# Block-sparse attention before a routed expert layer: K, Q and V loads issued by ScalarE, gathers issued in two halves, the last ranking step asked for later

## The chip, the cores and the metric

The kernel runs on one core of a Trainium2 chip. The metric is the device time of one execution in microseconds (us), as a median of several runs. The engines are called by these names: PE is TensorE (matmuls, and transposes by a matmul with the identity), DVE is VectorE, ACT is ScalarE, POOL is GpSimd and SP is SyncE, which here only issues transfers. ACT and POOL can issue transfers too. An engine's name with a "q" behind it (SPq) means its instruction queue: the issuing of transfers and the waits ahead of it.

## The reference

All data are float32. First comes block-sparse attention over B = 4 batches, H = 8 heads, S = 768 positions of D = 64 numbers, in blocks of 32 positions. A block of queries sees its own block and the two beside it, the first and the last block of the sequence, and three blocks drawn at random (`sampled_blocks`); queries of the first and last block see everything:

```
scores = where(mask, q @ k.T / sqrt(64), -1e9)
attn   = exp(scores - max); attn /= sum + 1e-9
x      = (attn @ v), heads side by side        # 3072 tokens x 512
```

Then comes a mixture of 8 experts in which each token goes to one expert, chosen by cosine similarity:

```
logits = (x / |x|) @ (emb / |emb|).T / tau
e, gate = argmax(logits), softmax(logits)[argmax]
out    = gate * (relu(x @ w1[e]) @ w2[e])      # w1 512 x 1024, w2 1024 x 512
```

## The kernel before

**Chunks and steps.** The attention is worked off in 24 chunks of 128 queries, six for each batch (`NC` = 6). `attention_fast` (L1206) has a loop over steps s from 0 to 24 (from L1266); b and c are batch and chunk within the batch. Each step scores chunk s, weighs the values of chunk s-1, and makes the logits of chunk s-2. A batch's K and V come in while the batch before is worked on.

In one step PE does, in this order: `score_near` (L502, tile `ac`, L521: scores against the neighbours and the end blocks), `score_far` (L532, tile `dps`, L543: scores against the random blocks), one half of `weigh_near` for chunk s-1 (tile `av`, L578), `turn_x` (L669, tile `xg_ps`), for c from 1 to 4 `turn_k` of one pair of heads of the next batch (L447, tile `kps`, L454, from the raw K rows `kraw`), `weigh_far` of chunk s-1 (L619; `av` out of `vg` and `pd`, L578), `turn_q` of chunk s+1 (L464, L469, from the raw Q rows `qraw`), `chunk_logits` of chunk s-2 (tile `yp`, L685), and the other half of `weigh_near`. In the first chunk of a batch `score_ends` (L553, tile `bps`, L565) is added. PE runs this list strictly in order.

ACT makes the exponentials (`pac` of `ac`, L525 and L529; four of `pd` out of `dps`, L548), every second copy of `kps` (L456), the squares of x (L666) and the copies of the logits (L686). DVE copies the turned Q (L473) and x (L676), part of the gathered K, and normalizes. POOL copies the gathered K (`kg`, L486) and near values into `vg` (L444).

**Loads.** SP issues nearly all transfers, in program order:

- `load_k` (L389) brings the K rows of one pair of heads as two transfers of 192 KB into one of two buffers of `kraw`. In the loop the step with chunk c of batch b loads pair c of batch b+1, which `turn_k` needs in step s+1.
- `load_q` (L380) brings the Q rows of chunk s+3 (256 KB; two transfers where c is 0) into one of three buffers `qraw`. Only the first two chunks' loads stand on ACT.
- `load_v` (L397) names eight parts of the next batch's V; two are loaded in each step with c of 1 to 4.
- `gather_v` (L426, issued at L434) brings the random value blocks of chunk s+1: up to 12 transfers of 64 KB, each from a row offset that SP has read from the tile `offset` (L371) into registers. They go into one of three buffers `vg`; `weigh_far` reads it two steps after the gathers were asked for. In chunk 0 of a batch there are 6.
- Later the stores of x (L776, L782) and the expert weights (L1071).

The body of a step stood in this order: K of the next batch, Q of chunk s+3, all gathers of chunk s+1, V of the next batch, `keep_ends` (L409, a POOL copy) where c is 4, then the scores. The attention is recorded with a schedule by hand: on each engine the instructions stay in the order of the program. A transfer signals its landing on one of eight semaphores that go round over all transfers that SP and ACT issue.

**Experts' embedding and the last ranks.** `build_experts` (L209) is a generator. Its first two parts (square, power, reciprocal, scaling of the embedding) stood before the first gathers; the transposes come in step 1. After the attention, `expert_tiles` (L1368) runs over tiles of 128 tokens, `expert_tile` (L1108) doing two halves of the first product (`hp`, L1118) and the second product (`yp`, L1131). The tokens of the first two batches are dispatched early, the others late. `rank` (L787, product at L794) counts the places of the last batch's tokens; the generator `between` called it, with the first part of `dispatch_late` (L942), after the first expert tile.

Of the kernel before, what the change touches and what calls it, by code (L numbers as in the profile page):

```python
# [20 lines left out]
P = 128  # L21
B, H, S, D = 4, 8, 768, 64
BLK = 32
NB = S // BLK
NRAND = 3
# [8 lines left out]
NE = (EARLY * S - E * (G - 1) + G - 1) // G  # L34
# [331 lines left out]
def shifts(k, engine, s, c):  # L366

    blocks = blocks_of(c)
    key = engine, s, c
    if key not in k.shift:  # L370
        _, values = k.nc.values_load_multi_w_load_instructions(  # L371
            k.offset[0:1, s, NG * c + blocks[0]:NG * c + blocks[-1] + 1], engines=(engine,), min_val=0, max_val=S - BLK,
            skip_runtime_bounds_check_because="the block numbers are clamped to the blocks there are")
        if engine == mybir.EngineType.SP and s == NRAND - 1:
            return list(values)
        k.shift[key] = list(values)
    return k.shift[key]


def load_q(k, n):  # L380

    b, c = divmod(n, NC)
    k.raw["q", n] = t = k.ld.tile([P, H, D], F32, name="qraw", tag="qraw", bufs=3)
    src = k.q[b].rearrange("h s d -> s h d")
    for rows, lo in pieces(c):
        (k.nc.scalar if n < 2 else k.nc.sync).dma_start(out=t[rows], in_=src[lo:lo + rows.stop - rows.start])


def load_k(k, g, pool=None):  # L389

    b, j = divmod(g, NPAIR)
    k.raw["k", g] = t = (pool or k.ld).tile([P, NC, 2, D], F32, name="kraw", tag="kraw", bufs=2)
    for h in range(2):
        k.nc.sync.dma_start(out=t[:, :, h], in_=k.k[b, 2 * j + h].rearrange("(c p) d -> p c d", p=P))  # L394


def load_v(k, b):  # L397
# [11 lines left out]
def keep_ends(k, b):  # L409

    k.nc.gpsimd.tensor_copy(out=k.vg0[b % 2][D:P], in_=k.vst[b % 2][0:D, 0])


def blocks_of(c):

    return range(2 if c == 0 else 0, NG)
# [6 lines left out]
    return slice(lo, lo + BLK), tile // 2  # L423


def gather_v(k, n):  # L426

    b, c = divmod(n, NC)
    k.vg[n] = t = k.vg_ring[n % len(k.vg_ring)]
    src = k.v[b].rearrange("h s d -> s h d")  # L430
    for s in range(NRAND):
        lanes = slice(s * BLK, (s + 1) * BLK)
        for g, shift in zip(blocks_of(c), shifts(k, mybir.EngineType.SP, s, c)):
            k.nc.sync.dma_start(out=t[lanes, g, :, 0:D], in_=src[bass.ds(shift, BLK)])  # L434


def near_v(k, n):
# [768 lines left out]
def attention_fast(n, ctx):  # L1206
    def pool(name, bufs, **kw):
        return ctx.enter_context(n.tc.tile_pool(name=name, bufs=bufs, **kw))

    nc = n.nc  # L1210
    right = ExitStack()
    n.big, n.dp = pool("big_f", 2, space=PSUM), pool("dp_e", 1)
    n.ld, n.qp, n.gp, n.pp, n.pb_pool = pool("ld", 1), pool("qp", 2), pool("gp", 2), pool("pp", 2), pool("pb", 1)
    odd = pool("odd", 1)
    even = right.enter_context(n.tc.tile_pool(name="even", bufs=1, side="right"))
    setup = ExitStack()
    n.setup = setup.enter_context(n.tc.tile_pool(name="setup", bufs=1, side="right"))
    for i, kv in enumerate((even, odd)):
        n.kt[i] = kv.tile([P, NPAIR, S], F32, name=f"kt{i}")
        n.ke[i] = kv.tile([P, NPAIR, D], F32, name=f"ke{i}")  # L1220
        n.vst[i] = kv.tile([P, NC, H, D + 1], F32, name=f"vst{i}")
        n.vg0[i] = kv.tile([P, H, D + 1], F32, name=f"vg0{i}")
    n.zeros = None
    n.vg_ring = [n.gp.tile([P, NG, H, D + 1], F32, name=f"vg{i}", tag=f"vg{i}", bufs=1) for i in range(3)]
    n.qt_ring = [n.qp.tile([P, NPAIR, 2, P], F32, name=f"qt{i}", tag=f"qt{i}", bufs=1) for i in range(2)]
    load_block_ids(n)
    for g in range(NPAIR):
        if g % 2 == 0:
            load_q(n, g // 2)
        load_k(n, g, n.setup if g < 2 else None)  # L1230
    load_experts(n)
    for to, src in load_v(n, 0):
        nc.sync.dma_start(out=to, in_=src)
    warm_up(n, 10)
    for vg in n.vg_ring:
        nc.vector.memset(vg, 0.0)
    nc.scalar.activation(n.setup.tile([P, 1], F32, name="first_exp"), n.zeros[:, 0:1], ACT.Exp)
    build_ident(n)
    for i in range(2):
        nc.gpsimd.memset(n.vst[i][:, :, :, D:D + 1], 1.0)  # L1240
        nc.gpsimd.memset(n.qt_ring[i], 0.0)
    for vg in n.vg_ring:
        nc.gpsimd.memset(vg[:, :, :, D:D + 1], 1.0)
    build_choice(n)
    turn_q(n, 0)
    for g in range(NPAIR):
        turn_k(n, g)
        if g:
            score_ends(n, 0, g - 1)
    score_ends(n, 0, NPAIR - 1)  # L1250
    build_bias(n)
    gather_k(n, 0)
    n.half = n.const.tile([P, NC], F32, name="half")
    nc.vector.memset(n.half, 0.5)
    experts = build_experts(n)
    next(experts)
    next(experts)
    gather_v(n, 0)
    near_v(n, 0)
    keep_ends(n, 0)  # L1260
    zero = n.const.tile([1, XW], F32, name="zero")
    nc.gpsimd.memset(zero, 0.0)
    nc.sync.dma_start(n.x_dram[N:N + 1, :], zero)
    plan = []
    for s in range(NCH + 1):
        b, c = divmod(s, NC)  # L1266
        if c == 1 and b:
            plan = after_sequence(n, b - 1) + [p for p in plan if p[0] >= s]

        def planned(half):  # L1270
            for when, part, what in plan:
                if (when, part) == (s, half):
                    what()

        if s == 0:
            load_q(n, 2)
            for g in range(NPAIR, NPAIR + 2):
                load_k(n, g)
        if b + 1 < B and c >= 2 and NPAIR * (b + 1) + c < B * NPAIR:
            load_k(n, NPAIR * (b + 1) + c)  # L1280
        if s + 3 < NCH:
            load_q(n, s + 3)
        if s + 1 < NCH:
            gather_v(n, s + 1)
        if b + 1 < B and c:
            for to, src in load_v(n, b + 1)[2 * c - 2:2 * c]:
                nc.sync.dma_start(out=to, in_=src)
        if b + 1 < B and c == 4:
            keep_ends(n, b + 1)
        if s < NCH:  # L1290
            score_near(n, s)
            score_far(n, s)
        if s + 1 < NCH:
            gather_k(n, s + 1)
        planned(0)
        if s >= 1:
            weigh_near(n, s - 1, 0)
        if s == 1:
            next(experts)
        ends = range(NPAIR) if c == 0 and 0 < s < NCH else ()  # L1300
        for j in ends[0:2]:
            score_ends(n, s, j)
        if s >= 2:
            turn_x(n, s - 2)
        for j in ends[2:]:
            score_ends(n, s, j)
        if 1 <= c <= NPAIR and b + 1 < B:
            g = NPAIR * (b + 1) + c - 1
            turn_k(n, g)
        if s >= 1:  # L1310
            weigh_far(n, s - 1)
        if s + 1 < NCH:
            near_v(n, s + 1)
            turn_q(n, s + 1)
        if s >= 2:
            chunk_logits(n, s - 2)
        if s == 1:
            next(experts)
        if s >= 1:
            weigh_near(n, s - 1, 1)  # L1320
            normalize(n, s - 1)
        if s == 0:
            build_consts(n)
        if s == 1:
            setup.close()
        if s == NC * (B - 1):
            right.close()
            n.wp = n.wp_ctx.enter_context(n.tc.tile_pool(name="wp", bufs=1, side="right", reuse_waits="tile"))
        planned(1)
# [35 lines left out]
                        pass  # L1365


def expert_tiles(n, between=(), halfway=None, then=None, spread=None):  # L1368
    def first_late():
        if spread:  # L1370
            spread()
        fetch_rows(n, NE)

    between, n.scattered, n.stop = iter(between), None, NE + FULL
    for i in range(NE + FULL):
        if i + 2 == NE:
            for _ in between:
                pass
        fetch(n, i)
        if len(parts(i)) == 2:  # L1380
            mixed_tile(n, i)
        else:
            expert_tile(n, i, first_late if i == NE - 2 else None, *((halfway, then) if i == 0 else ()))
        next(between, None)


# [16 lines left out]
def fast(n):  # L1403
    n.rings, n.loads = {}, 0
    with ExitStack() as ctx:
# [11 lines left out]
        n.dp = pool("dp", 1, reuse_waits="tile")  # L1417
        n.wp2, n.hps = pool("wp2", 1, reuse_waits="tile"), pool("hps", 1, space=PSUM)

        def between():  # L1420
            rank(n, B - 1)
            n.late = dispatch_late(n)
            next(n.late)
            yield
            yield
            next(n.late)
            count_good(n)
            yield
# [4 lines left out]
                for _ in route(n, B - 1):  # L1433
                    pass

        expert_tiles(n, between(), partial(turn_x, n, NCH - 1), last_route, lambda: next(n.late))


def more(n):
# [106 lines left out]
```

## Time and profile before

| | us |
|---|---|
| median of 3 runs (669.15, 669.15, 664.85) | 669.15 |
| the profiled execution | 663.43 |
| its span in the trace | 661.7 |
| first `ac` of the attention | 19.60 |
| first expert matmul | 285.3 |
| PE busy in the span | 609.8 |
| PE busy between 19.60 and 285.30 | 231.1 |
| transfers: median from issue to landing, `vg` / `kraw` / `qraw` / `vst` | 2.9 / 4.6 / 4.4 / 3.8 |

The span is the time from the first to the last instruction; the 1.7 us around it are not in the trace. A line such as "PE kps L454 <- DMA kraw<-in_k_dram: 14.6, 5, 5.4" reads: PE, at line 454 (writing the tile `kps`), waited for the transfer from K in memory to the tile `kraw`, 14.6 us in total, 5 times, 5.4 us at the longest. In the table by windows a row gives the window, its length, the busy time and (in brackets) the number of instructions of PE, PEld (PE's weight loads), DVE, ACT and POOL, then the clock that was granted to PE (1.00 is full), the busy share of the transfer engines and GB/s. The steps begin, by their first `ac`, at 19.6, 25.9, 38.1, 47.1, 56.8, 72.5, 81.0, 94.0, 106.3, 114.7, 124.3, 136.8, 144.4, 159.3, 171.5, 180.2, 196.2, 208.3, 216.1, 228.2, 244.0, 251.5, 259.8 and 269.5 us (steps 0 to 23).

### The profile page before, as it was taken

The page shows a single profiled execution, that of the slowest core. Times are in us where ns is not written, and L with a number is a line of the kernel's source. Part 1 is how long each engine was busy: PE and PEld are TensorE (multiplying, and loading weights), DVE is VectorE, ACT ScalarE, POOL GpSimd, SP SyncE. Part 2 cuts the span into 40 slices and gives each one's busy share as a digit, 9 for nine tenths or more (in the row PEclk, how much of TensorE's full clock was granted, in tenths as well). Part 3 has the DMA queues.
Part 4 walks back from the last instruction along what each step waited for, and adds up shares of the span by engine and source line. Part 5 has one row for each costly group of instructions (what it writes and reads, how often), then busy time and mean ns, then how long its engine had stood idle before and what let it go on. Part 6 is the DMA issues. An engine that isn't in the chain of part 4 may idle for free.

```text
span 661.7 us, 21659 instructions
## 1 busy us (share of the span) xinstructions
PE 609.8 (92%) x9016; PEld 477.6 (72%) x9016; DVE 224.3 (34%) x661; ACT 119.0 (18%) x265; POOL 235.6 (36%) x446
## 2 busy tenths in 40 slices
PE   7797989898968889897999999999999999999995
PEld 4696979797967879785777666774666755766773
DVE  5663335542643657225810211112211211221210
ACT  2523243443224424200000000000000000000000
POOL 1762333543352436203023333344333343333332
PEclk7899789988978989888999999999999999999998
DMA  8856664766667666999999999899899998999711
GB/s 178 172 129 150 148 139 105 176 137 168 145 146 168 161 142 177 245 276 398 374 412 388 349 354 335 313 340 331 309 404 394 409 373 315 406 399 399 281 49 33
DMA packets 189758, 170.80 MB, mean 258 GB/s; under 512 B 150152, under 2 KB 150280, under 8 KB 186834
## 3 DMA queue, kind: packets, MB, share of 16 engines
q1 hardware_dynamic: 182338, 155.36, 73.9%
q0 software_dynamic: 5216, 13.43, 5.7%
q8 instruction: 73, 1.20, 0.8%
q10 hardware_dynamic: 2096, 0.52, 0.4%
q14 instruction: 35, 0.29, 0.1%
HBM read 156.65 MB, written 12.90 MB: 256 GB/s over the span
## 4 chain that ended last, share of the span: by engine, by line
PE 83%; DMA 4%; SPq 4%; issue 3%; DVE 2%; POOL 1%; ACT 1%; POOLq 0%; DVEq 0%; ACTq 0%
PE hp L1118 25%; PE yp L1131 24%; PE av L578 11%; PE dps L543 5%; DMA kraw<-in_k_dram 4%; PE ac L521 3%; PE yp L685 3%; SPq L434 3%; PE hp L1163 2%; PE yp L1183 2%; PE xg_ps L469 2%; PE kps L454 2%; PE bps L565 1%; PE xg_ps L674 1%; SPq L394 1%
## 5 line engine op out<-in xcount | busy, mean ns | idle before, releaser
L1118 PEld LDWEIGHTS hp<-xgt,w 128*128 128x128 f32 x1472 | 169.5, 194 | 10.2 <-issue 10.2
L1118 PE MATMUL hp<-xgt,w 128*128 128x128 f32 x1472 | 170.2, 277 | 0.0
L1131 PE MATMUL yp<-w,h 128*128 128x512 f32 x368 | 162.0, 592 | 0.0
L1131 PEld LDWEIGHTS yp<-w,h 128*128 128x128 f32 x368 | 68.1, 190 | 76.6 <-issue 76.3
L1042 POOL DMA_INDIRECT xg<-x_dram,quarter x88 | 88.6, 1007 | 30.1 <-issue 27.4
L1144 POOL DMA_INDIRECT out_dram<-y,slot_l x20 | 20.3, 1015 | 156.7 <-DVE y L1143 156.7
L486 POOL COPY kg<-kt 128x128 f32 x176 | 44.6, 296 | 77.1 <-issue 46.9
L1121 ACT ACTIVATE h<-hp 128x512 f32<-128x512 f32 x23 | 13.7, 597 | 289.4 <-PE hp L1118 289.4
L444 POOL COPY vg<-vst 32x520 f32<-32x520 f32 x80 | 49.6, 619 | 33.4 <-PE av L578 25.1
L1125 DVE TENSOR_SCALAR h<-hp 128x512 f32<-128x512 f32 x23 | 15.9, 691 | 133.5 <-PE hp L1118 133.5
L578 PE MATMUL av<-vst,pac 64*64 64x65 f32 x1056 | 49.0, 230 | 5.7 <-issue 5.4
L473 DVE COPY qt<-xg_ps 64x512 f32<-64x512 f32 x48 | 33.1, 689 | 61.8 <-PE xg_ps L469 61.0
L543 PE MATMUL dps<-qt,kg 128*64 128x64 f32 x1408 | 49.6, 231 | 0.4 <-issue 0.4
L1143 DVE TENSOR_SCALAR y<-yp,gate 128x512 f32<-128x512 f32 x20 | 15.0, 751 | 102.2 <-PE yp L1131 90.1
L543 PEld LDWEIGHTS dps<-qt,kg 128*64 128x64 f32 x1408 | 46.1, 145 | 2.4 <-issue 0.7
L578 PEld LDWEIGHTS av<-vst,pac 64*64 64x64 f32 x1056 | 41.0, 141 | 5.3 <-issue 3.1
L548 ACT ACTIVATE pd<-dps,bias 128x256 f32<-128x256 f32 x88 | 34.6, 473 | 9.0 <-PE dps L543 8.5
L521 PE MATMUL ac<-qt,ke 64*64 64x128 f32 (+1 forms) x384 | 30.6, 292 | 4.3 <-DVE qt L473 3.8
L578 PE MATMUL av<-vg,pd 128*32 128x65 f32 x1408 | 29.7, 238 | 4.5 <-issue 4.3
L676 DVE COPY xt<-xg_ps 128x512 f32<-128x512 f32 x24 | 16.5, 689 | 44.2 <-PE xg_ps L674 44.2
L578 PEld LDWEIGHTS av<-vg,pd 128*32 128x32 f32 x1408 | 24.8, 120 | 9.1 <-issue 8.3
L454 PE MATMUL kps<-ident,kraw 128*128 128x128 f32 x96 | 16.3, 316 | 15.5 <-DMA kraw<-in_k_dram 15.5
(229 smaller groups left out, 645.8 us busy)
## 6 DMA issues: line engine op xcount, KB each, us to landing
w<-in_moe_w_dram SPq DMA_DIRECT2D x52, 2048.0 KB, 14.5
vg<-in_v_dram SPq DMA_DIRECT2D x264, 64.0 KB, 2.9
kraw<-in_k_dram SPq DMA_DIRECT2D x32, 192.0 KB, 4.6
vst<-in_v_dram SPq DMA_DIRECT2D x20, 256.0 KB, 3.8
qraw<-in_q_dram SPq DMA_DIRECT2D x19, 256.0 KB, 4.4
w<-in_moe_w_dram SPq DMA_DIRECT2D x8, 512.0 KB, 5.4
x_dram<-x SPq DMA_DIRECT2D x4, 774.0 KB
x_dram<-x SPq DMA_DIRECT2D x4, 516.0 KB, 9.6
```

Of the source, the lines that this page charges most:

```text
L444: k.nc.gpsimd.tensor_copy(out=k.vg[n][NRAND * BLK:P, g], in_=k.vst[b % 2][rows, m])
L454: nc.tensor.transpose(ps[:, c // 3, c % 3 * P:(c % 3 + 1) * P], raw[:, c].rearrange("p h d -> p (h d)"), k.ident)
L473: k.nc.vector.tensor_copy(out=t[rows, :, h], in_=ps[rows])
L486: copy(out=t[:, :, g, s * BLK:(s + 1) * BLK], in_=kt[:, :, bass.ds(shift, BLK)])
L521: nc.tensor.matmul(ps[D * r:D * (r + 1), h, lo:lo + cols.stop - cols.start], lhsT=keys, rhs=qt[rows, j, h, cols], start=True, stop=True)
L543: nc.tensor.matmul(out[D * r:D * (r + 1), NG * j + g], lhsT=kg[:, j, g, D * r:D * (r + 1)], rhs=qt[:, j, :, cols], start=True, stop=True)
L548: nc.scalar.activation(e[:, :, g].rearrange("p j h t -> p j (h t)"), out.rearrange("p (j g) h t -> p j g (h t)", g=NG)[:, :, g], ACT.Exp, ...
L578: k.nc.tensor.matmul(av[lanes, h // NPAIR, h % NPAIR * P:h % NPAIR * P + D + 1], lhsT=lhsT, rhs=rhs, start=first[0], stop=last, skip_group ...
L1042: k.nc.gpsimd.indirect_dma_start(out=x[:, g], out_offset=None, in_=quarters, in_offset=bass.IndirectOffsetOnAxis(ap=k.quarter[:, g, t:t + ...
L1118: nc.tensor.matmul(hp[:, f, :], lhsT=w1[:, d, (f0 + f) * P:(f0 + f + 1) * P], rhs=xt[:, d, :], start=(d == 0), stop=(d == ND - 1))
L1131: nc.tensor.matmul(yp, lhsT=h[:, f, :], rhs=w2[:, f, :], start=(f == 0), stop=(f == NF - 1))
L1144: k.scattered = nc.gpsimd.indirect_dma_start(out=k.out[:, :], out_offset=bass.IndirectOffsetOnAxis(ap=slot, axis=0), in_=y[:, :], in_offse ...
```

## The change

All K loads for batches 1 to 3, all Q loads, and the V loads within the loop are issued by ACT. In a step, `keep_ends` and the two scores come first, then the first half of the next chunk's gathers on SP, then the loads on ACT (in ACT's queue behind the exponentials of the scores), then the second half of the gathers. The two early parts of `build_experts` are asked for after `keep_ends` and after `build_consts`. The last batch's ranks and the first part of the late dispatch are asked for after the first half of the second expert tile's first product.

```diff
--- before.py
+++ after.py
@@ -383,7 +383,7 @@
     k.raw["q", n] = t = k.ld.tile([P, H, D], F32, name="qraw", tag="qraw", bufs=3)
     src = k.q[b].rearrange("h s d -> s h d")
     for rows, lo in pieces(c):
-        (k.nc.scalar if n < 2 else k.nc.sync).dma_start(out=t[rows], in_=src[lo:lo + rows.stop - rows.start])
+        k.nc.scalar.dma_start(out=t[rows], in_=src[lo:lo + rows.stop - rows.start])
 
 
 def load_k(k, g, pool=None):
@@ -391,7 +391,7 @@
     b, j = divmod(g, NPAIR)
     k.raw["k", g] = t = (pool or k.ld).tile([P, NC, 2, D], F32, name="kraw", tag="kraw", bufs=2)
     for h in range(2):
-        k.nc.sync.dma_start(out=t[:, :, h], in_=k.k[b, 2 * j + h].rearrange("(c p) d -> p c d", p=P))
+        (k.nc.scalar if b else k.nc.sync).dma_start(out=t[:, :, h], in_=k.k[b, 2 * j + h].rearrange("(c p) d -> p c d", p=P))
 
 
 def load_v(k, b):
@@ -423,15 +423,17 @@
     return slice(lo, lo + BLK), tile // 2
 
 
-def gather_v(k, n):
+def gather_v(k, n, part):
 
     b, c = divmod(n, NC)
     k.vg[n] = t = k.vg_ring[n % len(k.vg_ring)]
     src = k.v[b].rearrange("h s d -> s h d")
-    for s in range(NRAND):
-        lanes = slice(s * BLK, (s + 1) * BLK)
-        for g, shift in zip(blocks_of(c), shifts(k, mybir.EngineType.SP, s, c)):
-            k.nc.sync.dma_start(out=t[lanes, g, :, 0:D], in_=src[bass.ds(shift, BLK)])
+    todo = [(s, i, g) for s in range(NRAND) for i, g in enumerate(blocks_of(c))]
+    half = len(todo) // 2
+    todo = todo[half:] if part else todo[:half]
+    at = {s: shifts(k, mybir.EngineType.SP, s, c) for s in sorted({s for s, _, _ in todo})}
+    for s, i, g in todo:
+        k.nc.sync.dma_start(out=t[s * BLK:(s + 1) * BLK, g, :, 0:D], in_=src[bass.ds(at[s][i], BLK)])
 
 
 def near_v(k, n):
@@ -1253,11 +1255,11 @@
     n.half = n.const.tile([P, NC], F32, name="half")
     nc.vector.memset(n.half, 0.5)
     experts = build_experts(n)
-    next(experts)
-    next(experts)
-    gather_v(n, 0)
+    gather_v(n, 0, 0)
+    gather_v(n, 0, 1)
     near_v(n, 0)
     keep_ends(n, 0)
+    next(experts)
     zero = n.const.tile([1, XW], F32, name="zero")
     nc.gpsimd.memset(zero, 0.0)
     nc.sync.dma_start(n.x_dram[N:N + 1, :], zero)
@@ -1272,6 +1274,13 @@
                 if (when, part) == (s, half):
                     what()
 
+        if b + 1 < B and c == 4:
+            keep_ends(n, b + 1)
+        if s < NCH:
+            score_near(n, s)
+            score_far(n, s)
+        if s + 1 < NCH:
+            gather_v(n, s + 1, 0)
         if s == 0:
             load_q(n, 2)
             for g in range(NPAIR, NPAIR + 2):
@@ -1280,17 +1289,11 @@
             load_k(n, NPAIR * (b + 1) + c)
         if s + 3 < NCH:
             load_q(n, s + 3)
-        if s + 1 < NCH:
-            gather_v(n, s + 1)
         if b + 1 < B and c:
             for to, src in load_v(n, b + 1)[2 * c - 2:2 * c]:
-                nc.sync.dma_start(out=to, in_=src)
-        if b + 1 < B and c == 4:
-            keep_ends(n, b + 1)
-        if s < NCH:
-            score_near(n, s)
-            score_far(n, s)
+                nc.scalar.dma_start(out=to, in_=src)
         if s + 1 < NCH:
+            gather_v(n, s + 1, 1)
             gather_k(n, s + 1)
         planned(0)
         if s >= 1:
@@ -1321,6 +1324,7 @@
             normalize(n, s - 1)
         if s == 0:
             build_consts(n)
+            next(experts)
         if s == 1:
             setup.close()
         if s == NC * (B - 1):
@@ -1365,7 +1369,7 @@
                         pass
 
 
-def expert_tiles(n, between=(), halfway=None, then=None, spread=None):
+def expert_tiles(n, between=(), halfway=None, then=None, second=None, spread=None):
     def first_late():
         if spread:
             spread()
@@ -1380,7 +1384,7 @@
         if len(parts(i)) == 2:
             mixed_tile(n, i)
         else:
-            expert_tile(n, i, first_late if i == NE - 2 else None, *((halfway, then) if i == 0 else ()))
+            expert_tile(n, i, {1: second, NE - 2: first_late}.get(i), *((halfway, then) if i == 0 else ()))
         next(between, None)
 
 
@@ -1417,10 +1421,12 @@
         n.dp = pool("dp", 1, reuse_waits="tile")
         n.wp2, n.hps = pool("wp2", 1, reuse_waits="tile"), pool("hps", 1, space=PSUM)
 
-        def between():
+        def last_rank():
             rank(n, B - 1)
             n.late = dispatch_late(n)
             next(n.late)
+
+        def between():
             yield
             yield
             next(n.late)
@@ -1433,7 +1439,7 @@
                 for _ in route(n, B - 1):
                     pass
 
-        expert_tiles(n, between(), partial(turn_x, n, NCH - 1), last_route, lambda: next(n.late))
+        expert_tiles(n, between(), partial(turn_x, n, NCH - 1), last_route, last_rank, lambda: next(n.late))
 
 
 def more(n):
```

## The prediction

> **What bounds the kernel now.** I read the page's engines and its chain first, then the attention stretch in the table by windows, then the waits, then one step in the timeline.
>
> ```profile
> span 661.7 us, 21659 instructions
> PE 609.8 (92%) x9016; PEld 477.6 (72%) x9016; DVE 224.3 (34%) x661; ACT 119.0 (18%) x265; POOL 235.6 (36%) x446
> PE 83%; DMA 4%; SPq 4%; issue 3%; DVE 2%; POOL 1%; ACT 1%; POOLq 0%; DVEq 0%; ACTq 0%
> PE hp L1118 25%; PE yp L1131 24%; PE av L578 11%; PE dps L543 5%; DMA kraw<-in_k_dram 4%; PE ac L521 3%; PE yp L685 3%; SPq L434 3%; PE hp L1163 2%; PE yp L1183 2%; PE xg_ps L469 2%; PE kps L454 2%; PE bps L565 1%; PE xg_ps L674 1%; SPq L394 1%
> ```
>
> TensorE is the bound, and besides it the chain holds the K transfer and SP's issuing of gathers (L434). Windows split attention (first `ac` to first expert matmul) from experts:
>
> ```profile
> 19.60:285.30 265.70, 231.07 (x6645) 213.05 (x6641) 126.70 (x421) 94.97 (x218) 112.75 (x303) 0.91 0.68 156
> 285.30:661.70 376.40, 364.09 (x2153) 254.91 (x2152) 85.36 (x212) 17.30 (x32) 118.56 (x125) 0.99 0.89 334
> ```
>
> The first columns are length and PE's busy time. Attention leaves PE idle 34.6 us; the change touches little else. The waits within attention:
>
> ```profile
> PE kps L454 <- DMA kraw<-in_k_dram: 14.6, 5, 5.4
> PE av L578 <- issue: 9.7, 7, 3.1
> PE av L578 <- DMA vg<-in_v_dram: 0.2, 1, 0.2
> ```
>
> Five waits for K make 14.6 us (3.8, 0.6, 2.6, 5.4, 2.2, in steps 4, 9, 10, 15, 16). Gathered V is nearly always there in time: one wait, 0.2 us. That last line is what I expect to change most. SP's own waits in attention hold two lines that matter:
>
> ```profile
> SPq L434 <- DMA w<-in_moe_w_dram: 3.3, 3, 1.2
> SPq L434 <- DMA qraw<-in_q_dram: 0.8, 1, 0.8
> ```
>
> A gather reads neither a weight nor Q, yet it waits for them to land. The transfers of SP and ScalarE share eight completion semaphores in turn, and each transfer waits until the one before it on its semaphore has landed. While SP issues all of them, the one before is always older on the same queue, and such waits cost 4.1 us in all.
>
> One step (the third, step 2; the columns are start, length, engine, operation):
>
> ```profile
> 40.32 1.51 PE L543 MATMUL dps<-qt,kg 128*64 128x64 f32 x46
> 40.44 5.55 SPq L434 DMA_DIRECT2D vg<-in_v_dram  x8
> ...
> 42.06 1.55 ACT L548 ACTIVATE pd<-dps,bias 128x256 f32<-128x256 f32 x4
> ...
> 43.37 0.82 PE L454 MATMUL kps<-ident,kraw 128*128 128x128 f32 x6
> ...
> 44.12 1.12 PE L578 MATMUL av<-vg,pd 128*32 128x65 f32 x64
> ...
> 47.08 0.48 SPq L394 DMA_DIRECT2D kraw<-in_k_dram  x1
> 47.09 0.13 PEld L521 LDWEIGHTS ac<-qt,ke 64*64 64x64 f32 x1
> ```
>
> Far scores end at 41.83, the last of four far exponentials starts at 43.12, the far weighing of the previous chunk starts at 44.12, the next step at 47.09.
>
> **The change part by part.** *Loads to ScalarE.* SP loses two K, one or two Q and two V issues a step (0.48 to 0.65, 0.40 to 0.77 and 0.44 us each: about 2.6 us) and keeps 12 gathers of 0.50 us. ScalarE gets those 2.6 us; it is busy 95 of 265.7 us, so by itself that costs nothing; without that slack 24 steps by 2.6 us would be 62. But where do they stand? ScalarE works in order: at 40.52 its square started after a wait of 7.72 us, and an instruction of its queue for the next line stands at 40.53, though what that one waited for had long ended. So the loads go out when the last `pd` starts, 1.3 us after the far scores.
>
> *The semaphores.* The built program shows the order in which the eight semaphores are handed on. It is not the order in which SP and ScalarE reach their instructions. The last gather of chunk 1, on SP, waits for a K load that ScalarE issues in step 2; and the far weighing of chunk 1 on PE, also in step 2, waits for that gather. The same knot (gathers of chunk s-1 behind a K or Q load of step s) stands in steps 2, 3, 4, 5, 6, 9, 10, 14, 15 and 17. The chain in such a step, from the end of the far scores: 1.3 us to the last `pd`; 0.5 to the second K issue; K landing, 3.3 (25.65 to 28.93), 3.9 (61.00 to 64.86) or 4.6 (median of the page); the gather's landing, 1.9 to 2.9 (least and median). Taking 3.9 and, between 2.5 (64.65 to 67.12) and 2.9, 2.6: 8.3 us. Ends: 7.0 (3.3 and 1.9) and 9.8 (4.6, 2.9 and one more issue of 0.5 for Q). The matmuls left meanwhile are near weighing, turn of x and turn of K, 41.83 to 44.12, or 2.3 us; so PE stands about 6.0 us. Behind the waiting gather on SP stand the next gathers, the stores of x and, from 260 us, the first expert weights; the knots end at step 17, some 50 us of steps before these weights, so they are not late.
>
> Such a step is then 3.2 (`ac` and `dps`, 56.80 to 59.96) + 8.3 + 3.0 (44.12 to 47.09) = 14.5 us, and the clock comes on top. After the K wait of step 4 the window 65.60 to 72.50 has a granted clock of 0.50, and the work that took 3.7 us in step 2 (43.37 to 47.09) took 6.9 there: 3.2 more. The shortest slow stretch in the records is 3.4 us, half of it lost: 1.7. I take 1.7, since it is the commoner: 16.2 us; ends 13.2 (no slow clock, 7.0) and 19.2 (3.2 and 9.8). The ten steps took 9.0, 9.7, 15.6, 8.5, 13.0, 9.6, 12.5, 8.7, 16.0 and 7.7 = 110.3 us before. After: 162, so +51.7; ends +21.7 and +81.7. The K waits of four of them are in that difference already. Two more steps: step 16 loses its K wait and slow clock (2.2 + 1.7 = -3.9); step 1 gets about +3.6, since gathers of chunks 0 and 1 wait for loads of step 0 on ScalarE (one K landing of 3.9 less the cover; ends 0 and 7). Sum: +51.4 us.
>
> The Trainium skill speaks against the change's idea here ("DMA: Bandwidth & Descriptors", section "Issuing engines are not separate DMA queues": issuing from several engines saves only the sequencer's time, the transfers interleave on the same engines). By that alone the sum would be at best the K waits, -14.6 us and the clock; the two SP lines above show a coupling beyond it, which the built order makes the rule. The same page ("Why a DMA increments its semaphore by 16 and not by 1") asks for one semaphore per transfer in flight; that is where such a wait comes from, and the trace shows its price only as those 4.1 us.
>
> *Scores ahead of loads, gathers in halves.* On PE the order of instructions is the same in both builds, and on DVE and POOL but for the early norms. SP's offset loads move together (0.30 us each). Nothing: SP's first gathers leave up to 2.6 us sooner, and gathers cost PE 0.2 us before. If that cover is gone, it is the chain above.
>
> *The norms of the experts.* A square on ScalarE, a power on POOL (0.58 us) and three small DVE operations (0.8 us in all) move from before the first gather into step 0. They stand ahead of nothing that ends later than the first K; between -0.6 and +0.8 us, I take 0.
>
> *The last ranks.* On PE the product L794 still stands ahead of the second tile's matmuls, so its wait of 3.57 us (306.4 to 310.0) stays. Between -3.6 and +1 us; 0, since the order is the same.
>
> The profiled execution took 663.4 us (span 661.7 and 1.7 around it), 0.9% under the median of 669.15. 663.4 + 51.4 = 714.8; I say 715. By the ends (step 16 and step 1 with theirs) 681 to 748.
>
> **The rivals.** *Faster.* If ScalarE's queue issued transfers while its exponentials still wait, the loads would go out as soon as their buffer is free, the gathers behind them would land in time, and all K waits would go: 14.6 + 5 x 1.7 = 23 us, 640. For it: in the first 2.4 us both queues issue side by side, 0.41 to 0.65 us each. Against it: the instruction at 40.53. It decides where the chain is under 11.0 (the mean of the ten steps before) - 3.2 - 3.0 = 4.8 us without a slow clock; its least end is 7.0.
>
> *Half the chain.* The loads land fast and only five or six of the ten knots bind, because in the rest SP is late itself (12 gathers take it 7.4 to 10.7 us). For it: SP's lateness made the K waits. About half of 51: 690. Against: SP is relieved of 2.6 us a step.
>
> *ScalarE blocked longer.* V loads in a step wait for the step's first K load on their semaphore, so ScalarE stands some 4 us behind `pd` and is late with the K copy (0.81 us) and the next exponentials, in batches 0 to 2. Before, the copy followed `kps` with no delay. 5 to 8 steps by 4 us: 735 to 747. Against: PE waits for the gathers at that time anyway.
>
> *Nothing.* The two knots and the K waits gone cancel (ten steps by 2.5 us against 23): 665.
>
> **How the numbers follow.** Chain as worked out 0.58 (681 to 748), half 0.11, ScalarE blocked 0.13, nothing 0.04, faster 0.14. The range leaves out the faster case and a little: 672 to 745. A measurement of this kernel tells about 1% from no change, 6.7 us. Faster 0.14, same 0.05, slower 0.81.
>
> **What would show it.** Right: PE's wait for `vg` in far weighing goes from 0.2 to some 60 us, SP's wait at the gathers for `kraw` or `qraw` to as much, ScalarE's loads stand just behind the start of the last `pd`, steps 2 to 5 take 15 to 18 us, the expert tiles stay, K waits are gone. Wrong: loads on ScalarE well before `pd`; gathers landed before far weighing; steps of 8 to 9 us. If the first expert matmul starts before 285 the chain is refuted; if after 310 but with other waits, only its place.

## The result, and the profile after

| | before | after |
|---|---|---|
| median, us | 667.16 (4 runs, 664.85 to 669.15) | 721.86 (4 runs, 720.06 to 725.25) |
| span of the profiled execution | 661.7 | 723.5 |
| first `ac` to first expert matmul | 265.7 | 327.1 |
| of it PE busy / idle | 231.1 / 34.6 | 259.9 / 67.2 |
| first expert matmul to the end | 376.4 | 377.2 |

The changed kernel takes 1.083 times as long (95% interval 1.0765 to 1.0889): 55 us more between the medians, 61.8 between the two spans. The forecast was 715, in a range of 672 to 745. All of the loss lies in the attention, half of it idle time of PE (+32.6 us) and half of it busy time of a slower PE (+28.8). The windows of the changed kernel (columns as before):

```profile
19.20:346.30 327.10, 259.88 (x6644) 238.29 (x6641) 124.06 (x421) 94.94 (x218) 112.36 (x303) 0.82 0.59 127
346.30:723.50 377.20, 364.98 (x2154) 255.81 (x2152) 85.47 (x212) 17.30 (x32) 118.52 (x125) 0.99 0.90 333
```

The number of matmuls in the attention is the same, their busy time is not, and the granted clock beside it fell from 0.91 to 0.82. The chain of the page, by engine and by line:

```profile
PE 77%; DMA 12%; issue 3%; SPq 2%; ACT 2%; DVE 2%; POOL 1%; ACTq 0%; POOLq 0%; DVEq 0%
PE hp L1120 23%; PE yp L1133 22%; PE av L580 11%; DMA vg<-in_v_dram 5%; PE dps L545 4%; DMA kraw<-in_k_dram 4%; PE yp L687 3%; PE ac L523 3%; PE xg_ps L471 2%; PE hp L1165 2%; PE yp L1185 2%; SPq L436 2%; DMA qraw<-in_q_dram 1%; PE bps L567 1%; PE xg_ps L676 1%
```

The transfers' share has tripled, and gathers of V (`vg`) stand in it now. The single transfer is not slower: the median from issue to landing is 3.0 us for a gather (2.9 before) and 3.2 for a K load (4.6 before). What PE waits for in attention, and below it what SP waits for:

```profile
PE av L580 <- DMA vg<-in_v_dram: 33.1, 12, 6.0
PE av L580 <- issue: 11.3, 7, 4.2
PE av L580 <- DMA vst<-in_v_dram: 11.0, 2, 6.0
```

```profile
SPq L436 <- DMA kraw<-in_k_dram: 82.0, 15, 10.8
SPq L436 <- DMA qraw<-in_q_dram: 34.9, 13, 8.8
SPq L436 <- DMA vst<-in_v_dram: 6.0, 8, 1.4
```

PE's wait for K at `kps` is gone from the list; the wait for gathered V went from 0.2 us to 33.1 (and 11.0 more are booked on V loads). SP, at the line of the gathers, stands 117 us for K and Q, which no gather reads. Step 2, from the far scores on:

```profile
40.12 1.69 PE L545 MATMUL dps<-qt,kg 128*64 128x64 f32 x52
...
42.03 0.46 ACT L550 ACTIVATE pd<-dps,bias 128x256 f32<-128x256 f32 x1
42.10 0.39 ACTq L394 DMA_DIRECT2D kraw<-in_k_dram  x1
42.38 0.47 ACT L550 ACTIVATE pd<-dps,bias 128x256 f32<-128x256 f32 x1
42.54 0.56 ACTq L394 DMA_DIRECT2D kraw<-in_k_dram  x1
...
43.74 2.67 ACTq L1294 DMA_DIRECT2D vst<-in_v_dram  x2
43.84 0.31 PE L580 MATMUL av<-vg,pd 128*32 128x65 f32 x6
46.45 0.80 ACT L458 COPY kt<-kps 128x768 f32<-128x768 f32 x1 [2.86 <-DMA qraw<-in_q_dram]
46.59 5.98 SPq L436 DMA_DIRECT2D vg<-in_v_dram  x10
50.15 1.94 PE L580 MATMUL av<-vg,pd 128*32 128x65 f32 x58 [5.99 <-DMA vg<-in_v_dram]
```

Read it from the bottom: far weighing stops after six matmuls and resumes at 50.15. It needs chunk 1's last gather, which SP issues at 46.59, 4.05 us after ScalarE issued the second K load (42.54), when that has landed. The chain of the profile has the same three links (start, length, what):

```profile
42.54 4.04 DMA kraw<-in_k_dram
46.59 3.51 DMA vg<-in_v_dram
50.15 1.94 PE av L580 x58
```

The rest of the weighing takes 1.94 us for 58 matmuls, where all 64 took 1.12 before.

### The profile page after: what moved, and what is told of

Its sections match the earlier page's. It is cut to its first block, busy times and chain, and to the rows that moved or that the text cites. A ratio compares the mean times of both kernels' runs of the same rounds, so it can differ in the third digit from the quotient of the medians.

```text
span 723.5 us, 21705 instructions
## 1 busy us (share of the span) xinstructions
PE 639.0 (88%) x9016; PEld 503.6 (70%) x9016; DVE 222.0 (31%) x661; ACT 118.9 (16%) x265; POOL 235.6 (33%) x446
## 4 chain that ended last, share of the span: by engine, by line
PE 77%; DMA 12%; issue 3%; SPq 2%; ACT 2%; DVE 2%; POOL 1%; ACTq 0%; POOLq 0%; DVEq 0%
PE hp L1120 23%; PE yp L1133 22%; PE av L580 11%; DMA vg<-in_v_dram 5%; PE dps L545 4%; DMA kraw<-in_k_dram 4%; PE yp L687 3%; PE ac L523 3%; PE xg_ps L471 2%; PE hp L1165 2%; PE yp L1185 2%; SPq L436 2%; DMA qraw<-in_q_dram 1%; PE bps L567 1%; PE xg_ps L676 1%
## 5 line engine op out<-in xcount | busy, mean ns | idle before, releaser
L580 PE MATMUL av<-vg,pd 128*32 128x65 f32 x1408 | 43.5, 268 | 52.6 <-DMA vg<-in_v_dram 33.1
L580 PEld LDWEIGHTS av<-vg,pd 128*32 128x32 f32 x1408 | 34.3, 139 | 61.1 <-issue 30.6
L475 DVE COPY qt<-xg_ps 64x512 f32<-64x512 f32 x48 | 33.1, 689 | 116.3 <-PE xg_ps L471 115.6
L580 PE MATMUL av<-vst,pac 64*64 64x65 f32 x1056 | 52.5, 246 | 1.1 <-issue 0.8
L580 PEld LDWEIGHTS av<-vst,pac 64*64 64x64 f32 x1056 | 44.6, 156 | 6.3 <-issue 4.2
L550 ACT ACTIVATE pd<-dps,bias 128x256 f32<-128x256 f32 x88 | 34.6, 474 | 15.5 <-PE dps L545 15.4
L523 PE MATMUL ac<-qt,ke 64*64 64x128 f32 (+1 forms) x384 | 35.3, 324 | 1.3 <-DVE qt L475 1.3
L523 PE MATMUL ac<-qt,kt 64*64 64x64 f32 x704 | 34.7, 259 | 0.0
L580 PE MATMUL av<-vg,pac 64*64 64x65 f32 x352 | 31.8, 254 | 2.3 <-issue 2.3
```

Source lines behind the costliest of these rows:

```text
L475: k.nc.vector.tensor_copy(out=t[rows, :, h], in_=ps[rows])
L523: nc.tensor.matmul(ps[D * r:D * (r + 1), h, lo:lo + cols.stop - cols.start], lhsT=keys, rhs=qt[rows, j, h, cols], start=True, stop=True)
L550: nc.scalar.activation(e[:, :, g].rearrange("p j h t -> p j (h t)"), out.rearrange("p (j g) h t -> p j g (h t)", g=NG)[:, :, g], ACT.Exp, ...
L580: k.nc.tensor.matmul(av[lanes, h // NPAIR, h % NPAIR * P:h % NPAIR * P + D + 1], lhsT=lhsT, rhs=rhs, start=first[0], stop=last, skip_group ...
```

## The experiments

The theory: the order in which the eight semaphores are handed on makes gathers of SP wait for loads that ScalarE issues one or two steps later. Rival A: a second issuing engine costs by itself (its own time, or two queues side by side). Rival B: the new order within a step costs. Ratios are against the kernel before, on the same chip, with 95% intervals.

### e1: only the order of the semaphores

```diff
+    def behind(ins, c):
+        if c in n.last_gather:
+            n.tc.add_manual_dep(ins, n.last_gather[c].name, mybir.DependencyInfo(
+                mybir.DependencyClass.Sync, mybir.DependencyReason.DATA), reason="order of loads")
...
-                nc.scalar.dma_start(out=to, in_=src)
+                n.behind(nc.scalar.dma_start(out=to, in_=src).ins, s - 1)
```

The K and Q loads get the same edge. It is a wait of its own, too: a load of step s now leaves only when the last gather of chunk s-1 has landed.

> The changed kernel with every load on ScalarE where the change put it; the only edit is that each load of step s also waits for the last gather of chunk s-1 to have landed, which hands the eight semaphores on in an order where no gather stands behind a load of a later step than the one its values are needed in (12 such pairs in the changed kernel, none here). Theory (gathers wait for loads through the shared semaphores): the waits of far weighing for vg fall from 44 us to under 10 and the time to 640 to 672, since the K waits stay gone. Rival A (ScalarE's issuing, or the two queues side by side, is what costs): still 700 to 725, since both stay. Rival B (the order within a step costs): still 700 to 725.

664.95 us, ratio 1.0019 (0.9977 to 1.006). With the loads still on ScalarE, in the same place of the program, the whole loss is gone. SP still stands 55.1 us at its gathers for K and Q (28.9 and 26.2, 116.9 in the changed kernel), but few of these waits now reach PE. PE's longest waits in e1:

```profile
PE av L584 <- issue: 9.2, 8, 2.0
PE yp L800 <- ACT lg L692: 5.5, 2, 3.0
PE av L584 <- DMA vg<-in_v_dram: 4.7, 8, 1.6
PE dps L549 <- issue: 4.4, 3, 3.3
PE bps L571 <- ACT pb L574: 4.2, 2, 2.9
```

The K waits are gone here too, and yet nothing is won: PE stands idle 38.8 us in the attention against 34.6 before. Two of the new lines end with ScalarE (9.7 us): its own work now stands behind its loads, which wait in turn (its copy of `kps` stood 12.0 us for K loads that it does not read). With the 4.7 us for `vg` these lines are 14.4 us, in the place of 14.6 for K. So ScalarE is not free of cost as an issuer in this run; how much of that comes from the edge itself, which holds its loads back, is not shown.

### e2, e3, e4: which loads

```diff
-        k.nc.scalar.dma_start(out=t[rows], in_=src[lo:lo + rows.stop - rows.start])
+        (k.nc.scalar if n < 2 else k.nc.sync).dma_start(out=t[rows], in_=src[lo:lo + rows.stop - rows.start])
...
-        (k.nc.scalar if b else k.nc.sync).dma_start(out=t[:, :, h], in_=k.k[b, 2 * j + h].rearrange("(c p) d -> p c d", p=P))
+        k.nc.sync.dma_start(out=t[:, :, h], in_=k.k[b, 2 * j + h].rearrange("(c p) d -> p c d", p=P))
...
-                nc.scalar.dma_start(out=to, in_=src)
+                nc.sync.dma_start(out=to, in_=src)
```

All three edits make e2; e3 leaves the one on K out, e4 the one on V.

> The changed kernel with all loads on SP, in the new place between the halves of the gathers and behind the scores in the program; norms and last ranks as in the change. Theory: one queue, so no pair of gather and later load; the K loads stand behind six gathers (3 us), so K waits of 15 to 30 us: 660 to 685. Rival A (ScalarE as issuer costs): about 667. Rival B (scores ahead of loads and gathers in halves cost): 700 to 725.

664.96 us, ratio 1.0011 (0.9976 to 1.0046). Scores ahead of loads and gathers in halves neither cost nor bring anything; rival B falls. Between the theory and rival A this run does not decide: both allow 665.

> The changed kernel with only the K loads on ScalarE; Q and V on SP between the halves. In this build 11 gathers stand behind a K load of a later step, in steps 3, 4, 5, 9, 10, 11 and 15. Theory: far weighing waits in just these seven steps, 4 to 6 us each, K waits gone: 695 to 715. Rival A (ScalarE's issuing time costs, in proportion to its loads: 24 of 69): 680 to 690 with small waits in all steps. Rival B (order): 700 to 725 with no step singled out.

691.01 us, ratio 1.0375 (1.0322 to 1.0427): 4 us under the range, but the seven steps are those named; one more, step 23, waits 2.7 us. The waits in the seven are 2 to 4.3 us, smaller than expected. Steps 3, 4, 5, 9, 10, 11 and 15 take 14.1, 17.3, 17.1, 14.1, 14.5, 17.1 and 16.7 us; step 14, which the full change makes 18.0, takes 8.4. Rival A has no reason for that choice.

> The changed kernel with only the V loads on ScalarE; K and Q on SP between the halves. One gather stands behind a V load of a later step, in step 3. Theory: as with all loads on SP but for step 3: 660 to 690. Rival A (ScalarE's issuing time; 15 of the large loads): 675 to 690. Rival B (order): 700 to 725.

695.88 us, ratio 1.047 (1.0405 to 1.0536): outside all that I expected but rival B, which e2 excludes. I had counted only gathers that stand behind a load of two steps later. SP's waits in e4 show what that misses:

```profile
SPq L436 <- DMA vst<-in_v_dram: 42.2, 11, 12.6
SPq L386 <- DMA vst<-in_v_dram: 17.2, 3, 8.8
SPq L394 <- DMA vst<-in_v_dram: 5.6, 1, 5.6
```

Gathers that stand behind a V load of just the next step block SP's queue, and here K loads stand behind them in that queue: PE waits 34.2 us for K, in four waits of up to 10.0. The mechanism is the theory's; the load that comes too late is another.

### e5 and e9: loads ahead of the scores

```diff
-        if b + 1 < B and c == 4:
-            keep_ends(n, b + 1)
-        if s < NCH:
-            score_near(n, s)
-            score_far(n, s)
-        if s + 1 < NCH:
-            gather_v(n, s + 1, 0)
...
         if s + 3 < NCH:
             load_q(n, s + 3)
+        if s + 1 < NCH:
+            gather_v(n, s + 1, 0)
+            gather_v(n, s + 1, 1)
...
                 nc.scalar.dma_start(out=to, in_=src)
+        if b + 1 < B and c == 4:
+            keep_ends(n, b + 1)
+        if s < NCH:
+            score_near(n, s)
+            score_far(n, s)
         if s + 1 < NCH:
-            gather_v(n, s + 1, 1)
             gather_k(n, s + 1)
```

This is e9. In e5 the last line but one was not taken out, so that the second half of the gathers stood twice.

> All K, Q and V loads of the loop on ScalarE as in the change, but in their former place, ahead of the scores of their step, and the gathers in one piece between Q and V as before; norms and last ranks as in the change. ScalarE reaches the loads some 4 us earlier in each step than in the changed kernel, but 28 gathers instead of 12 now stand behind a load of two steps later. Theory (the order in which the eight semaphores are handed on): no better for the earlier issue, 700 to 770, with far weighing waiting for vg in nearly all steps of batches 0 to 2. Rival (the place behind the exponentials is what costs): 640 to 672.

779.34 us, ratio 1.1776 (1.1682 to 1.1871), with 393 gathers in place of 264.

> As e5 was meant: K, Q and V loads of the loop on ScalarE ahead of the scores of their step, 12 gathers a step, between Q and V as before; norms and last ranks as in the change. (In the kernel of e5, and in that of e7, the second half of each chunk's gathers stood twice, so these two measured 6 more gathers a step.) 28 gathers stand behind a load of two steps later. Theory: 700 to 750 with waits for vg in most steps of batches 0 to 2. Rival (the place behind the exponentials costs): 640 to 672.

717.94 us, ratio 1.0778 (1.071 to 1.0845), as slow as the change, though the loads go out earlier in the step. The place behind the exponentials is not the cause.

### e6: loads at the end of the step

```diff
-        if s + 3 < NCH:
-            load_q(n, s + 3)
...
-                nc.scalar.dma_start(out=to, in_=src)
...
+        if s + 3 < NCH:
+            load_q(n, s + 3)
...
+                nc.scalar.dma_start(out=to, in_=src)
         planned(1)
```

The K loads move with them.

> The changed kernel with the loads at the end of their step's program, on ScalarE behind the copy of the logits and the square; gathers of both halves together. No gather stands behind a load of two steps later, 36 stand behind one of the next step. That load now goes out when the next step but one has begun, lands 4 us later and the gather 2.6 after that, while far weighing comes 5 to 6 us into the step. Theory, with e4 in mind (distance counts as time, not as steps): waits of 2 to 5 us in most steps of batches 0 to 2, 690 to 740. Rival (only pairs at a distance of two steps cost): 645 to 672.

716.1 us, ratio 1.0779 (1.071 to 1.0848), with 35.0 us of waits of far weighing for `vg` in 19 waits. No gather stands behind a load of two steps later here. So that distance is not needed for the loss; together with e1, where gathers still wait but land in time, this speaks for the time at which the gather lands, not for a number of steps.

### e7 and e12: norms and last ranks alone

```diff
-    next(experts)
-    next(experts)
-    gather_v(n, 0)
+    gather_v(n, 0, 0)
+    gather_v(n, 0, 1)
     near_v(n, 0)
     keep_ends(n, 0)
+    next(experts)
...
             build_consts(n)
+            next(experts)
...
-            expert_tile(n, i, first_late if i == NE - 2 else None, *((halfway, then) if i == 0 else ()))
+            expert_tile(n, i, {1: second, NE - 2: first_late}.get(i), *((halfway, then) if i == 0 else ()))
```

The two halves of each chunk's gathers stand one right behind the other, as one piece. In e7 the second half stood twice, as in e5: 393 gathers.

> The kernel before with only the two small parts of the change: the norms of the experts' embedding in step 0, and the last ranks asked for in the second expert tile. All loads on SP in their former place and order. Theory: nothing, 660 to 672, with the wait of the rank product at 3.6 us as before. Rival (the norms or the ranks cost or bring something): outside 657 to 675.

729.02 us, ratio 1.0974 (1.0903 to 1.1045). That says nothing on norms or ranks, but it prices SP: 129 more gathers made 65.6 us, 0.51 each, about SP's own rate of one per 0.50 us. Not all of it is standing still: PE's busy time in the attention is 257.3 us, 26.2 more than before, at a clock of 0.85. The chain of e7 has SP's issuing of gathers at 18%, 3% before:

```profile
PE hp L1120 23%; PE yp L1133 22%; SPq L436 18%; PE av L580 4%; DMA vg<-in_v_dram 2%; PE hp L1165 2%; PE yp L1185 2%; SPq L371 2%; PE yp L687 1%; DMA w<-in_moe_w_dram 1%; SPq L386 1%; SPq L1290 1%; SPq L394 1%; PE dps L545 1%; DMA kraw<-in_k_dram 1%
```

> As e7 was meant: the kernel before, all loads on SP in their former place and 12 gathers a step, with only the norms of the experts' embedding in step 0, the last ranks asked for in the second expert tile, and SP's offset loads drawn together. Theory: nothing that can be measured, 659 to 672; the rank product waits 3.6 us as before. Rival (one of these parts costs or brings something): outside 657 to 675.

666.04 us, ratio 1.0002 (0.9964 to 1.004); the rank product waits 3.6 us for POOL, as before and after.

### e8, e10, e11: another issuer with semaphores of its own

```diff
-        k.nc.sync.dma_start(out=t[:, :, h], in_=k.k[b, 2 * j + h].rearrange("(c p) d -> p c d", p=P))
+        (k.nc.gpsimd if b else k.nc.sync).dma_start(out=t[:, :, h], in_=k.k[b, 2 * j + h].rearrange("(c p) d -> p c d", p=P))
```

This is e8, on the kernel before. e11 has `g > NPAIR + 1` in place of `b`. e10 is the changed kernel with `k.nc.gpsimd` in place of `k.nc.scalar` for all loads in the loop.

> The kernel before with only the K loads of batches 1 to 3 issued by POOL, whose transfers signal on semaphores of their own; Q, V and gathers on SP as before. Theory: no gather can stand behind a K load, SP is relieved of two issues a step, and the K waits go unless POOL is late: 640 to 668. Rival A' (a second issuing engine costs by itself, here POOL's time for each transfer, about 1 us by its indirect rows, ahead of the copies into kg and vg): 675 to 720 with waits of dps for kg.

655.18 us, ratio 0.9887 (0.9808 to 0.9966). At `kps`, where PE waited 14.6 us for K, 0.8 us of waiting is left.

> The changed kernel, every load where the change put it, but issued by POOL in place of ScalarE (K of batches 1 to 3, Q from chunk 2 on, V in the loop). POOL's transfers signal on other semaphores. Theory (the shared semaphores are the cost): no waits of gathers for loads, 640 to 675, POOL's own 0.82 us for each transfer (5 to 6 a step, 4 to 5 us) the only new cost. Rival A (a second issuer, or loads behind the scores, cost by themselves): 700 and more.

673.53 us, ratio 1.0105 (1.0054 to 1.0155). Seven eighths of the loss are gone with no edit but the issuer, so neither the place of the loads nor a second issuer is the cause, and rival A falls as the main one. No gather waits for a K, Q or V load any more (82.0, 34.9 and 6.0 us in the changed kernel). What is left of the loss probably comes from POOL, though no run shows it alone: it waits 61.7 us for buffers of `qraw`, its copies into `vg` and `kg` stand behind that, and PE waits 3.5 us for `kg`.

> As e8, K loads on POOL, but the first four (two pairs of batch 1, asked for in step 0) stay on SP: in e8 POOL issued them from 24.5 to 28.3 us ahead of the gathered K, and PE waited 3.6 us for Q's copy and the next step began later (step 2 at 40.1 instead of 38.1). Theory: the K waits stay gone and 2 us come back: 648 to 656. Rival (e8's start was not late because of them): 655 to 660.

654.45 us, ratio 0.9843 (0.9799 to 0.9887): the fastest, clear of both kernels. The windows of e11 and, below, POOL's issues of K:

```profile
19.00:272.00 253.00, 224.81 (x6644) 205.41 (x6640) 130.42 (x420) 95.20 (x218) 129.31 (x324) 0.96 0.72 162
```

```profile
L394 POOL DMA_DIRECT2D kraw<-in_k_dram x20 | 17.0, 851 | 27.6 <-PE kps L454 27.6
```

The attention is 12.7 us shorter than before, the granted clock 0.96 against 0.91, for 17.0 us of POOL's time. The reason I gave for it was wrong in part: step 2 begins at 37.5 us, 2.5 earlier than in e8, but the wait for Q's copy is still there (3.8 us in three waits, as in the kernel before). The intervals of e8 and e11 overlap.

## Why the prediction was right, and where its terms were off

**The pairs of gather and load** were read from the built program, and e1 shows them to be the cause: by the ratios to the kernel before (1.083 and 1.002) the order is worth 8.1%, some 54 us. e10 says nearly the same without e1's extra wait. Of the ten steps named, nine stall at far weighing by 2.5 to 6.8 us (in step 17 and for part of step 3 the profile names no releaser); step 6 does not. Its chunk is a batch's first, with `score_ends` ahead of far weighing, which begins 5.8 us after the far scores there (110.30 to 116.14) instead of 2.3; I had not counted that cover. Step 21, which I had not named, stalls for 3.5 us and takes 15.2 us instead of 8.3. SP stands 6.8 us at its gathers for Q loads between 284 and 313 us, and the chain into this stall runs through its issuing of gathers. So SP's queue seems to carry the wait on to later gathers, a path that the forecast does not have.

**The steps' sum** came out well: 17.5, 20.1, 17.9, 14.5, 12.0, 18.6, 16.4, 18.0, 18.2 and 12.6 make 165.8 us, against the 162 forecast. The terms within did not, so that the sum came out well is in part luck:

- *The chain of 8.3 us.* In step 2 it is 8.34 (41.81 to 50.15), but made otherwise. ScalarE issued its first load at 42.10, as the first `pd` had started, not the last, so 1 us fell away. Seven of the ten steps are like that (0.01 to 0.07 us after the first `pd`); in steps 14 and 6 the first load left 0.34 and 1.15 us before the first `pd` had started, and only in step 9 behind the last, 1.57 us after the first. So exponentials that wait behind one another mostly do not hold a transfer back. In step 2 the gather's landing took 3.51 us, not 2.6. Over all ten steps PE stalls 45 us, not 60; SP's waits for K and Q, forecast to be as long, are 117.
- *The half clock of 1.7 us for a stall* is the term that was mis-sized. PE's busy time in attention grew by 28.8 us; I had 10 x 1.7 for the new stalls less 5 x 1.7 for the old, 8.5. By 28.8 + 8.5 it is about 3.7 us for each of ten stalls (an estimate), above even the 3.2 that I had set aside as the less common. After the stall of step 2 the weighing (1.94 us for 58 matmuls), the tail (3.43 us from the end of far weighing to the next step, 1.85 before) and the scores of step 3 (4.83 us, 3.38 before) are all slow, and step 3 as a whole ran at a clock of 0.67. The two errors, 15 us of idle time too much and 20 us of slow clock too little, nearly cancel.

```profile
38.00:55.50 17.50, 11.27 (x259) 10.30 (x259) 5.58 (x18) 4.06 (x9) 5.01 (x13) 0.80 0.51 115
55.50:75.70 20.20, 13.36 (x269) 12.18 (x269) 5.13 (x15) 3.37 (x8) 3.79 (x11) 0.67 0.56 102
```

Step 3 holds 13.36 us of PE's work here; the same step took 9.7 us in all before. Followed in short windows, the granted clock is either 1.00 or 0.50, so its mean gives the time at half clock: 0.82 over 327.1 us is some 118 us, 0.91 over 265.7 us some 48 us before. One such stretch of the kernel before, which begins late in the K wait of 3.8 us, and two of the changed kernel, which begin late in the stalls of steps 2 and 3:

```profile
64.10:74.20 10.10, 8.58 (x155) 8.08 (x158) 2.38 (x6) 1.46 (x4) 1.61 (x5) 0.50 0.56 125
48.70:58.80 10.10, 8.65 (x169) 8.34 (x170) 3.52 (x13) 1.55 (x4) 3.08 (x5) 0.50 0.28 63
65.70:79.40 13.70, 9.88 (x182) 9.16 (x184) 3.52 (x13) 1.80 (x4) 1.85 (x3) 0.50 0.61 102
```

The trace of the kernel before could have told it: there the K waits of 2.2 and 2.6 us each come with 3.4 us of half clock, those of 5.4 and 3.8 us with stretches of 6.8 and 10.1. The shortest stretch was the commonest, but it belonged to short waits, and the stalls forecast were 6 us long.

**Step 16** gained 2.0 us of the 3.9 forecast, step 1 lost 2.8 of 3.6. In the two profiled executions the attention is 61.4 us longer, 10 more than the 51.4 forecast: 3.8 of it in the ten steps, 7.0 in step 21, and the rest of the steps nearly cancel. The medians are only 54.7 us apart, because the profiled execution before was below its median and the one after above. **Order, halves, norms, ranks**, taken at nothing, are nothing (e2, e12).

**The rivals.** *Faster* failed where it was said to decide: ScalarE's transfers do pass exponentials that wait behind one another, but in the ten steps none left before the far scores of its step had ended, and the chain (8.34 us in step 2) stayed far above 4.8 us. *ScalarE blocked* is real but small: in step 2 ScalarE's copy of `kps` stood 2.86 us behind the loads while PE waited for the gather anyway, and in e1 such waits seem to be what keeps the K waits from being won. What the expectation for e4 missed is that the queue behind a waiting gather can carry the wait to K. K loads alone (e3) or V loads alone (e4) are enough for a loss; Q loads alone were not run.

The Trainium skill ("DMA: Bandwidth & Descriptors", section "Issuing engines are not separate DMA queues") says that issuing from several engines saves only the sequencer's time, usually small beside the transfer itself. Here one gather's issue is indeed small beside its transfer (0.50 us against 2.9 from issue to landing), but SP issues one behind the other, and it adds up: 65.6 us for the 129 more gathers of e7. e11, with 20 K issues on POOL instead of SP, is 11 us faster than the kernel before; its K loads also signal apart from SP's, so not all of that need be issuing time.

What stays open: step 6 of the forecast was settled only by its order of work, with no run of its own, and how far ScalarE's queue runs ahead of its waiting exponentials was seen in the rows (mostly three or four) but not tried.

## What to carry to other kernels

Before a transfer is moved to a second issuing engine, look whether the two share completion semaphores, and in which order the built program hands these on: a transfer that reads nothing of another can wait for it, and an in-order queue carries that wait to whatever stands behind. If an issuer's queue holds up the engine that bounds the kernel, give some of its transfers to an issuer with semaphores of its own (here K on POOL, 1.6% faster); more is not always better (K, Q and V on POOL, in the change's order of a step, 1% slower). Price the slow clock from a stall as long as the one forecast, not from the commonest stretch in the trace.

## What was not expected of the hardware

In seven of the ten steps ScalarE's first transfer left within 0.07 us of the start of the first of four exponentials, with three still to run, and in step 14 0.34 us before it; that is earlier than its order in the program suggests. Step 3, between two stalls, ran at 0.67 of the clock, and over the attention the slow clock cost nearly as much as standing still: +28.8 us busy beside +32.6 us idle. And SP, which the page never counts as busy, had next to no slack: 129 transfers of 64 KB more cost 65.6 us.
